# RWKV-6 attention and a gated MLP on one core: the first step's second chunk reads the first chunk by a seventh level

## The chip, the cores and the metric

The kernel runs on one core of a Trainium2 chip. Its time is the device time of one launch in microseconds (us); three runs of the kernel before gave 569.8 us as median, 569.65 at the lowest and 570.21 at the highest. The core has five engines with a queue of instructions each: TensorE (PE in the profile; its weight loads are PEld), VectorE (DVE), ScalarE (ACT), GpSimd (POOL), and SyncE (SP), which here issues DMA transfers. They wait for each other by semaphores only.

## The reference

Two blocks, one after the other. The attention has 4 sequences, 8 heads, 768 tokens and 48 channels a head, and carries a 48x48 state through the tokens:

```python
for t in range(S):
    cur = np.einsum('bhd,bhe->bhde', u[None] * kt, vt)
    y[:, :, t] = np.einsum('bhd,bhde->bhe', rt, state + cur)
    state = wt[:, :, :, None] * state + np.einsum('bhd,bhe->bhde', kt, vt)
```

Here rt, kt, vt and wt are token t of r, k, v and w, and the state starts at zero. The result, as 3072 rows of 384 numbers, goes through an MLP: `h = x @ w_in` (384 to 2048), `g = h * erf(softplus(h))`, and `g @ w_out` (2048 to 384). Everything is float32 here; a float32 matmul shows in the profile as two records.

## The kernel before

**Steps.** The work is cut into 12 steps. A step takes 128 tokens of two sequences, so 16 heads: r and k lie as `in[:, x, n]` (x = 0 for r, 1 for k), a tile of 128 partitions in which the even head e = 0 of pair n sits in partitions 0 to 47 and the odd head e = 1 in 64 to 111 (`rows(e)`), with the 128 tokens along the free dimension; n = 0 to 7, and j = 0, 1 is the sequence. The 128 tokens are two chunks of 64 (`HC`), called c or h = 0 and 1. In step 0 the tile is ordered by sequence first and read by `first_pair`.

**Levels.** Inside a chunk the decay between tokens s and t is built up by halves. At level l blocks of 2^l tokens are looked at: `level_products` (L712) multiplies k of every block's left half with r of its right half on PE into a PSUM bank (`pp`), `take_level` (L722, or L729 and L743 by ACT) moves the part that belongs to the level into the tile `own` (source token in the partitions, target token along the free dimension), and then `scale` (L357 and L364, DVE) multiplies r of the right halves by the total decay of the left halves and k of the left halves by that of the right halves, for the next level to use. POOL makes the totals (`plan_totals`, L397). Six levels finish a chunk of 64. PE's next level waits for the scaling of this one, and the scaling waits for this level's products, which read the same tile. `keep_busy` and `stay_warm` are matmuls whose results nobody reads.

**y and the state.** `from_own` (L756) multiplies `own` with v: a chunk's tokens over the same chunk, into the PSUM tile `y`. What chunk 1 takes from chunk 0 goes through the state: k is turned (transposes, L1023 in step 0, L1152 in the others), `state_part` (L829) multiplies the turned k with v, the result becomes `middle` (the state between the chunks), and `through_state` (L782) multiplies r of chunk 1 with `middle` into `y`. Then y is moved out: `y3` (L790), a matmul `hop` that puts the fourth part of y into free rows (L797, step 0), and copies into `xT` (L803). `xT` is what the MLP reads.

**The order in step 0 (`attend_first`, L950 to L1061).** After level 6, DVE scales k of both chunks (`scale_last(j, True)`, L374), PE turns k, then `from_own` of one half of y, ACT and DVE copy the turned k to `kT`, PE makes chunk 0's part of the state (`state_part(0, kT, ps, (0,))`), the other half of `from_own`, ACT and DVE copy it to `middle`, POOL fades it, PE runs `through_state`, ACT copies `y3`. Chunk 1's part of the state is made in step 1 by `pending`, between levels 2 and 3.

**Step 1 (`attend`, L1081).** Its PE order is written out: half of level 1, `hop`, the other half, then for each level a piece of the first step's MLP (L1242: two column blocks of x @ w_in, 12 records) after the level's products. The banks of PSUM for the products take turns (`products`, `turns["next"]`): level l + 1 uses the bank that level l - 1 used, and what `pending` writes at level l goes to the bank of level l + 1.

**The weights** come as 64-bit floats and are turned to 32 bits on the chip, in 16 pairs of rows: pair i is loaded into one of three buffers `words` ("l": two DMAs of 384 KB, SP; a small copy into the buffer, by ACT or POOL, sets when it may start), ACT makes the high part ("b", L289, for pairs 0 and 1 in PSUM tiles "m", of which there are two) and the low part ("r", L297), DVE shifts the high part ("h", L306) and POOL adds the two ("o", L319). Pair i of `w_in` must be ready for the i-th piece of L1242.

Everything around the change is issued in program order, engine by engine (a manual schedule); nothing is reordered.

## Time and profile before

| what | us |
|---|---|
| median of the three runs | 569.8 |
| the profiled execution's own time | 569.77 |
| its span | 568.0 |
| PE busy | 560.9 (99%) |
| DVE busy | 452.1 (80%) |
| ACT busy | 358.5 (63%) |
| POOL busy | 244.9 (43%) |
| DVE starts to scale behind level 6 of step 0 (L374) | 17.48 |
| `hop` starts (L797) | 23.08 |
| first MLP piece starts (L1242) | 25.26 |
| third MLP piece starts (L1242, in level 3 of step 1) | 33.62 |

The first three rows are times of a launch: the profiled execution took 569.77 us, 1.77 us more than the span in which its instructions lie. The busy rows are sums over that span. The last four rows are places in it, in us from its start, read from the chain of work that ended last: they follow the stretch that the change touches. PE is busy nearly everywhere; in the stretch from 17.9 to 22.6 us it was busy 3.92 of 4.70 us, from 25.3 to 48 us all the time.

### The profile page before, as it was taken

The numbers are of one execution on the slowest core, as the hardware profiler recorded it, in microseconds if no ns is written. First come the engines' busy times: TensorE is split into PE (matmuls) and PEld (weight loads), VectorE is DVE, ScalarE is ACT, GpSimd is POOL, SyncE is SP. The second block draws the span as 40 slices with busy tenths as digits, with TensorE's granted clock in tenths as the row PEclk, the third lists the DMA queues.
The fourth block names the chain that finished last, engine by engine and source line by source line (L and its number), as shares of the span: only waits on it lengthen the run. The fifth ranks groups of instructions, "written<-read, shape, count | busy, mean of one in ns | idle before, by whom it ended". The sixth has DMA issues, their size and how long they took to land.

```text
span 568.0 us, 16706 instructions
## 1 busy us (share of the span) xinstructions
PE 560.9 (99%) x7314; PEld 499.7 (88%) x7314; DVE 452.1 (80%) x511; ACT 358.5 (63%) x496; POOL 244.9 (43%) x262
## 2 busy tenths in 40 slices
PE   8999999999999999999999999999999999999997
PEld 6788886588988998998998998998899899989997
DVE  8895886999899898798798789689689487477720
ACT  3777787556458858747757766765676771589500
POOL 3785482533885883393484185176072000000000
PEclk9999999999999999999999999999999999999999
DMA  8793753350435325145145235235232201000000
GB/s 268 238 383 143 256 194 117 129 155 3 147 119 136 111 95 146 25 170 167 23 145 181 36 135 188 39 113 167 48 112 84 47 9 36 2 2 0 29 29 28
DMA packets 54081, 63.24 MB, mean 111 GB/s; under 512 B 35160, under 2 KB 40568, under 8 KB 52984
## 3 DMA queue, kind: packets, MB, share of 16 engines
q1 hardware_dynamic: 53480, 61.98, 34.5%
q8 instruction: 57, 0.93, 0.7%
q10 hardware_dynamic: 528, 0.20, 0.1%
q14 instruction: 16, 0.13, 0.1%
HBM read 52.39 MB, written 8.69 MB: 108 GB/s over the span
## 4 chain that ended last, share of the span: by engine, by line
PE 87%; DVE 7%; issue 3%; POOL 1%; ACT 1%; DVEq 0%; POOLq 0%; ACTq 0%
PE m L1364 33%; PE m L1242 31%; PE c L1467 6%; PE pp L712 5%; PE y L756 2%; PE m L1274 2%; PE y L782 2%; DVE in L364 2%; PE pp L829 2%; PE m L1067 1%; PE pp L1076 1%; POOL w_out_sb L1305 1%; DVE h L1207 1%; DVE own L722 1%; PE pp L1152 1%
## 5 line engine op out<-in xcount | busy, mean ns | idle before, releaser
L1242 PE MATMUL m<-xT,w_in_sb 128*128 128x256 f32 x960 | 214.6, 381 | 0.3 <-ACT h L1251 0.2
L1242 PEld LDWEIGHTS m<-xT,w_in_sb 128*128 128x128 f32 x960 | 180.1, 190 | 25.5 <-ACT h L1251 0.6
L364 DVE TENSOR_TENSOR in<-in,tot_sb 128x1024 f32<-128x1024 f32 (+1 forms) x55 | 77.5, 1409 | 6.6 <-PE pp L712 6.2
L1251 ACT COPY h<-m 128x512 f32<-128x512 f32 x80 | 46.2, 579 | 52.2 <-PE m L1242 52.0
L1364 PE MATMUL m<-mixed,h 128*128 128x192 f32 x320 | 56.7, 331 | 0.0
L1364 PE MATMUL m<-w_out_sb,h 128*128 128x192 f32 x320 | 56.1, 329 | 0.0
L1364 PEld LDWEIGHTS m<-mixed,h 128*128 128x128 f32 x320 | 51.8, 190 | 0.8
L1364 PEld LDWEIGHTS m<-w_out_sb,h 128*128 128x128 f32 x320 | 52.0, 190 | 0.5
L1364 PE MATMUL m<-w_out_sb,room 128*128 128x192 f32 x288 | 49.7, 326 | 0.0
L1364 PEld LDWEIGHTS m<-w_out_sb,room 128*128 128x128 f32 x288 | 47.3, 190 | 0.1
L1202 ACT ACT_TABLE_LOAD x28 | 35.9, 1283 | 8.7 <-DVE h L1207 6.7
L514 POOL TENSOR_TENSOR words<-words,own 128x384 f32<-128x384 f32 x21 | 29.8, 1418 | 26.3 <-DVE words L545 13.6
L712 PEld LDWEIGHTS pp<-in 48*48 48x48 f32 (+4 forms) x2368 | 30.2, 120 | 10.9 <-issue 6.0
L555 POOL TENSOR_TENSOR words<-words 128x384 f32<-128x384 f32 x28 | 38.7, 1410 | 0.0
L507 POOL TENSOR_TENSOR own<-rest 128x384 f32<-128x384 f32 x7 | 8.1, 1152 | 69.1 <-ACT o L1370 69.1
L1198 ACT ACT_TABLE_LOAD x28 | 35.9, 1283 | 1.8 <-issue 1.3
L712 PE MATMUL pp<-in 48*48 48x32 f32 (+4 forms) x2368 | 34.1, 206 | 0.2 <-DVE in L364 0.2
L459 POOL TENSOR_TENSOR tot_sb<-tot_sb 128x256 f32<-128x256 f32 (+4 forms) x50 | 30.9, 618 | 3.8
L580 DVE TENSOR_REDUCE sums<-rk 128x16 f32<-128x768 f32 (+2 forms) x31 | 31.3, 1022 | 0.0
L555 POOL TENSOR_TENSOR rk<-words 128x384 f32<-128x384 f32 x28 | 30.6, 1122 | 0.0
L1198 ACT ACTIVATE room<-h 128x1024 f32<-128x1024 f32 x28 | 29.6, 1057 | 0.3
L319 POOL TENSOR_TENSOR w_out_sb<-w_out_sb,rest 128x768 int32<-128x768 int32 x8 | 18.0, 2254 | 21.6 <-DVE w_out_sb L311 21.5
(222 smaller groups left out, 1007.0 us busy)
## 6 DMA issues: line engine op xcount, KB each, us to landing
in<-in_rkw SPq DMA_DIRECT2D x8, 1024.0 KB, 5.4
words<-in_moe_w_in SPq DMA_DIRECT2D x16, 384.0 KB, 6.0
words<-in_moe_w_out SPq DMA_DIRECT2D x16, 384.0 KB, 4.6
words<-in_rk_rows SPq DMA_DIRECT2D x8, 768.0 KB, 6.0
w<-in_rkw SPq DMA_DIRECT2D x11, 512.0 KB
v<-in_v SPq DMA_DIRECT2D x12, 384.0 KB, 5.6
out<-o SPq DMA_DIRECT2D x23, 192.0 KB, 4.0
in<-in_rkw SPq DMA_DIRECT2D x7, 512.0 KB, 5.7
```

The lines of the kernel that those rows point to most:

```text
L364: nc.vector.tensor_mul(halves, halves, view(tots[level - 1], 0, [[1, n], [2, nb], [0, half]]))
L459: nc.gpsimd.tensor_mul(new, pair[:, :, 0], pair[:, :, 1])
L514: engine.tensor_mul(to, to, of[:, :, None, :].to_broadcast([P, NEAR // 2 // half, half, D]))
L555: engine.tensor_mul(to[:, i], r[:, half:], k[:, part * rows + i, None].to_broadcast([P, half, D]),)
L580: nc.vector.tensor_reduce(out=to, in_=of, axis=mybir.AxisListType.X, op=ALU.add)
L712: nc.tensor.matmul(to, lhsT=rk(1, n)[rows(e), s0 : s0 + m], rhs=right, start=True, stop=True,)
L1198: nc.scalar.activation(sp_room, chunks[0], AF.Softplus)
L1202: nc.scalar.activation(at, sp_room, AF.Erf)
L1242: nc.tensor.matmul(ps[:, ff, :], lhsT=w_in_sb[:, g * FG + f + ff, kk * P : (kk + 1) * P], rhs=xT[:, kk, :], start=kk == 0, stop=kk == KT - 1,)
L1251: nc.scalar.copy(h[:, f : f + FT, :], ps[:])
L1364: nc.tensor.matmul(to, lhsT=a[:, f], rhs=b[:, f], start=start and f == 0, stop=f == FG - 1, skip_group_check=True,)
L1467: nc.tensor.matmul(to[:, f], lhsT=turns["weights"][b][:, i * FT + f], rhs=turns["tokens"][a], start=a + b in STARTS and not f, stop=True, ...
```

## The change

Step 0 no longer makes the state between its chunks. After level 6 it scales only what is needed next (k of chunk 0 for the first sequence, r of chunk 1 for all, k of chunk 0 for the second), and PE multiplies k of chunk 0 with r of chunk 1: a seventh level, 64x64 tokens for each of the 16 heads, into two "m" tiles (`far`), one for each e. `into_y` then takes the place of `from_own`, `state_part` and `through_state`: first y of chunk 0 over the 64 partitions of `own` that hold chunk 0; then DVE (e = 1) and ACT (e = 0) copy `far` over those 64 partitions, and y of chunk 1 is one matmul over all 128 partitions, chunk 0 and chunk 1 at once. k of chunk 1 is scaled behind that, and `move_last`, the second half of the old `through_state`, moves y out as before.

The transposes and both halves of the state go to step 1: at level 2 `pending` turns k and ACT copies it to `kT`; at level 3 it makes both halves of the state, DVE copies `middle`, POOL fades it, DVE adds the second half.

Weight pair 0 has its high part made in place in `w_in_sb`, in one instruction, so the "m" tiles are free for `far`. The loads of pairs 2 and 3 are set off by POOL instead of ACT: pair 2 behind level 6, pair 3 behind POOL's u products for step 1. `keep_busy` does three matmuls of 128 columns instead of one of 384, and `stay_warm` after level 1 does four of 128 instead of two of 256.

```diff
@@ -280,7 +274,9 @@
             if i not in held:
                 return
-            if i < 2:
+            if not i:
+                base = weights[i][0][:, part]
+            elif i < 2:
                 base = ps_m.tile([P, NP * C], FP32, name="m")[:, :DM]
             else:
                 base = y[:].rearrange("p e q j t -> p e (q j t)")[:, :, :DM]
...
@@ -365,15 +361,20 @@
             halves, halves, view(tots[level - 1], 0, [[1, n], [2, nb], [0, half]])
         )
-    def scale_last(batch, k):
-
-        half, nb = 1 << (LOG - 1), JP * C // NJ >> LOG
-        t, tots = turns["first"][:, batch], ready[0][1]
-        at, every, of = (NP * C, 1, 1) if k else (half + HC, NC, 2)
-        halves = view(t, at, [[2 * half * every, nb // every], [1, half]])
+    def scale_last(n, x, c):
+
+        half = 1 << (LOG - 1)
+        rk, tots = turns["first"], ready[0][1]
+        side = 1 - x
+        blocks = C // half
+        offset = (n.start // NP * 2 + x) * NP * C + n.start % NP * C + c * HC + side * half
+        many = n.stop - n.start > NP
+        dims = [[2 * NP * C, NJ], [C, NP]] if many else [[C, NP]]
+        halves = view(rk, offset, [*dims, [1, half]])
+        by = [[NP * blocks, NJ], [blocks, NP]] if many else [[blocks, NP]]
         nc.vector.tensor_mul(
             halves, halves,
-            view(tots[LOG - 1], 2 * batch * nb + of, [[2 * every, nb // every], [0, half]]),
+            view(tots[LOG - 1], n.start * blocks + NC * c + x, [*by, [0, half]]),
         )
     def plan_totals(s):
...
@@ -774,17 +775,21 @@
             if not (c or h):
                 continue
             t = slice(h * HC, (h + 1) * HC)
-            for j, q in ((0, 2), (1, 2), (1, 0), (0, 0)) if not s else np.ndindex(NJ, NP // 2):
-                q = q if not s else 2 * q
+            for j, q in np.ndindex(NJ, NP // 2):
+                q = 2 * q
                 for e in range(NE):
                     for p in (q + e, q + 1 - e):
                         n = j * NP + p
                         nc.tensor.matmul(
                             y[at(e, p), e, p // 2, j, t],
                             lhsT=state[rows(e), n, :],
-                            rhs=(in_t[:, 0, n] if s else first_pair(0, n))[rows(e), t],
+                            rhs=in_t[:, 0, n][rows(e), t],
                             start=False, stop=True, skip_group_check=True,
                         )
+
+        move_last(s, xT)
+
+    def move_last(s, xT):
         y3 = att.tile([P, UNIT], FP32, name="y3", bufs=1)
         nc.scalar.copy(y3[:].rearrange("p (j t) -> p j t", j=NJ), y[:, 1, 1])
...
@@ -961,7 +966,7 @@
         pp = products([P, NE, JP, HC])
         for half in halves:
             level_products(pp, by_pair(made), 1, half)
-        stay_warm(2)
+        stay_warm(4, 1)
         nc.scalar.copy(first[:], mask_sb[:, 0, :])
         for j in range(NJ):
             scale(0, 1, batch=j)
...
@@ -985,7 +990,7 @@
                 level_products(pp, first_pair, level, half)
                 scale(0, level, batch=j)
             turns["pp"] = products([P, NE, JP, HC])
-            keep_busy(turns["pp"], (DM,))
+            keep_busy(turns["pp"], (P,) * KT)
             (take_blocks if level == MASKED else take_level)(own, pp, level)
             wait_for(1 << level - 1)
             if level == 2:
...
@@ -993,8 +998,7 @@
             else:
                 totals(*behind[level])
             if level == 2:
-                stages["b"](0, 0)
-                stages["b"](0, 1)
+                stages["b"](0)
                 stages["r"](0)
                 nc.sync.dma_start(out=vt[:], in_=v[0])
             if level == 3:
...
@@ -1006,66 +1010,92 @@
                 nc.sync.dma_start(out=ws[1][:], in_=rkw[1][:, 2])
         totals = plan_totals(1)
         pp = turns.pop("pp")
-        for j, half in enumerate(halves):
+        all_n, (n0, n1) = slice(0, JP), (slice(j * NP, (j + 1) * NP) for j in range(NJ))
+        for half in halves:
             level_products(pp, first_pair, LOG, half)
-            scale_last(j, True)
-        got = pp[:].rearrange("p e n t -> p (e n) t")
-        half = HC // 2
-        for s0, copy in ((0, nc.scalar.copy), (HC, nc.vector.tensor_copy)):
-            copy(own[s0 : s0 + half, :, half:], got[s0 : s0 + half, :, :half])
+        scale_last(n0, 1, 0)
+        scale_last(all_n, 0, 1)
+        scale_last(n1, 1, 0)
+        far = [
+            ps_m.tile([P, NP * C], FP32, name="m")[:HC].rearrange("p (n t) -> p n t", n=JP)
+            for _ in range(NE)
+        ]
+        for n in range(JP):
+            for e in range(NE):
+                nc.tensor.matmul(
+                    far[e][:, n, :], lhsT=first_pair(1, n)[rows(e), :HC],
+                    rhs=first_pair(0, n)[rows(e), HC:], start=True, stop=True,
+                )
+        take_level(own, pp, LOG)
+        stages["l"](2, ready[0][1][LOG - 1][:, 0:1])
         wait_for(0, 1)
         next(second)
-
-        kT = att.tile([P, NH, D], FP32, name="kT", bufs=1)
-        turned = products([P, JP, P])
-        turns["next"] = 1 - turns["next"]
-        for n in range(JP):
-            nc.tensor.transpose(turned[:, n, :], first_pair(1, n), ident[:])
-        from_own(0, own, 1)
-        for e, copy in ((1, nc.scalar.copy), (0, nc.vector.tensor_copy)):
-            copy(kT[:, e * JP : (e + 1) * JP], turned[:, :, e * EP : e * EP + D])
-        for j in range(NJ):
-            scale_last(j, False)
-        fence()
-        stages["l"](2, seen[:, 0:1], True)
-        ps = [[products([P, NE, JP, HC], 1 - e)[:, e] for e in range(NE)]]
-        state_part(0, kT, ps, (0,))
-        from_own(0, own, 0)
-        nc.scalar.copy(middle[rows(1)], ps[0][1][rows(1), :, :D])
-        nc.vector.tensor_copy(middle[rows(0)], ps[0][0][rows(0), :, :D])
-        stages["l"](3, middle[:, 0, 0:1], True)
+        scale_last(all_n, 1, 1)
+
+        def into_y(h, e):
+
+            t = slice(h * HC, (h + 1) * HC)
+            of = slice(0, t.stop) if h else t
+            for j, q in np.ndindex(NJ, NP // 2):
+                for p in (2 * q, 2 * q + 1):
+                    n = j * NP + p
+                    nc.tensor.matmul(
+                        y[at(e, p), e, q, j, t],
+                        lhsT=vt[of, n * NE + e, :], rhs=own[of, e * JP + n, :],
+                        start=not (h or j or q), stop=True, skip_group_check=True,
+                    )
+
+        for e, copy in ((1, nc.vector.tensor_copy), (0, nc.scalar.copy)):
+            into_y(0, e)
+            copy(own[:HC, e * JP : (e + 1) * JP], far[e])
+        into_y(1, 1)
+        into_y(1, 0)
+        stages["l"](3, ready[1][0][:, 1, 0, 0:1])
         load_v(1)
         stages["h"](0)
-        stages["h"](0)
-        nc.gpsimd.tensor_mul(faded[1][:], middle[:], ends[:, :, 1:2].to_broadcast([P, JP, D]))
-        stages["o"](0)
-        through_state(0, xT)
         stages["b"](1, 0)
+        move_last(0, xT)
         stages["b"](1, 1)
         stages["r"](1)
+        stages["o"](0)
         stages["h"](1)
         stages["h"](1)
         totals(1)
         stages["o"](1)
         totals(2)
         turns["totals"] = lambda: totals(*range(3, LOG + 1))
-
-        def pending():
-            part = products([P, NE, JP, HC], turns["next"])[:, 0]
-            state_part(0, kT, ps + [[part] * NE], (1,))
-            nc.vector.tensor_add(S_next[both], faded[1][both], part[both, :, :D])
-            load_third()
-            stages["l"](5)
-            load_w(2)
+        kT = att.tile([P, NH, D], FP32, name="kT", bufs=1)
+
+        def pending(level):
+            if level == 2:
+                turned = products([P, JP, P], turns["next"])
+                for n in range(JP):
+                    nc.tensor.transpose(turned[:, n, :], first_pair(1, n), ident[:])
+                nc.scalar.copy(
+                    kT[:].rearrange("p (e n) d -> p e n d", e=NE),
+                    turned.rearrange("p n (e d) -> p e n d", e=NE)[..., :D],
+                )
+                loaded[2] = [ins.tile([P, 2, JP, C], FP32, name="in"), None]
+                stages["l"](5)
+                load_w(2)
+                return
+            both_halves = products([P, NC, JP, HC], turns["next"])
+            state_part(0, kT, [[both_halves[:, h]] * NE for h in range(NC)])
+            nc.vector.tensor_copy(middle[both], both_halves[both, 0, :, :D])
+            nc.gpsimd.tensor_mul(
+                faded[1][:], middle[:], ends[:, :, 1:2].to_broadcast([P, JP, D])
+            )
+            nc.vector.tensor_add(S_next[both], faded[1][both], both_halves[both, 1, :, :D])
+            loaded[2][1] = ins.tile([P, NH, D], FP32, name="v")
         turns["pending"] = pending
-    def stay_warm(times):
+    def stay_warm(times, wide=NC):
         for _ in range(times):
-            ps = ps_m.tile([P, NC, P], FP32, name="m")
+            ps = ps_m.tile([P, wide, P], FP32, name="m")
             nc.tensor.matmul(
-                ps[:], lhsT=ident[:], rhs=ident[:, None, :].to_broadcast([P, NC, P]),
+                ps[:], lhsT=ident[:], rhs=ident[:, None, :].to_broadcast([P, wide, P]),
                 start=True, stop=True,
             )
...
@@ -1105,8 +1135,8 @@
             if s == 1 and 2 < level:
                 stages["h"](level + 1)
             scale(s, level)
-            if s == 1 and level == 2:
-                turns.pop("pending")()
+            if s == 1 and level in (2, 3):
+                turns["pending"](level)
             if s == 1 and level == 2:
                 stages["h"](3)
             if s == 1 and level > 1:
```

## The prediction

> **What bounds the kernel now.** I read the page's busy shares first, then a table by stretches of time, then the chain that ended last around the change, then the timelines of DVE and POOL there.
>
> ```profile
> PE 560.9 (99%) x7314; PEld 499.7 (88%) x7314; DVE 452.1 (80%) x511; ACT 358.5 (63%) x496; POOL 244.9 (43%) x262
> ```
>
> PE is the bound: 7.1 us of 568.0 are left. So a change can gain only where PE idles, or by PE work that it takes away.
>
> ```profile
> 17.90:22.60 4.70, 3.92 (x150) 3.45 (x153) 3.64 (x10) 1.91 (x6) 2.69 (x6) 1.00 0.51 130
> 22.60:25.30 2.70, 2.69 (x71) 2.04 (x62) 1.93 (x4) 2.65 (x7) 2.70 (x3) 1.00 0.80 251
> 25.30:36.40 11.10, 11.10 (x200) 9.20 (x200) 9.67 (x10) 7.59 (x13) 9.51 (x11) 1.00 0.99 360
> 36.40:48.00 11.60, 11.60 (x263) 9.63 (x263) 9.94 (x9) 8.85 (x16) 10.22 (x11) 1.00 0.99 389
> ```
>
> The columns are the stretch, its length, then busy time of PE, PEld, DVE, ACT, POOL, the granted clock (1.00) and the DMA share. In the stretch that the change rewrites PE idles 0.78 us; where the state is to go it never idles, and DVE hardly does.
>
> The chain that ended last:
>
> ```profile
> 17.48 0.44 DVE in L374
> 17.92 0.14 issue
> 18.05 1.08 PE pp L1023 x8
> 19.16 0.49 ACT kT L1026
> 19.67 0.57 DVE kT L1026
> 20.28 0.88 PE pp L829 x30
> 21.25 0.54 DVE middle L1035
> 21.93 0.67 PE y L782 x32
> 22.60 0.47 PE pp L712 x32
> 23.08 1.56 PE y L797 x6
> ...
> 29.09 0.73 PE pp L829 x32
> ...
> 47.90 1.02 PE pp L1152 x8
> ...
> 51.52 0.86 PE pp L829 x64
> ```
>
> From level 6 to hop the work passes from engine to engine: turn, copy, state, copy, y. Behind hop the chain is PE alone. The rows at 47.90 and 51.52 are step 1's own transposes and state, and price the moved ones.
>
> ```profile
> 29.22 2.61 DVE L364 TENSOR_TENSOR in<-in,tot_sb 128x1024 f32<-128x1024 f32 x1 [0.98 <-PE pp L712]
> 31.75 0.54 DVE L1056 TENSOR_TENSOR s<-faded,pp 112x384 f32<-112x384 f32 x1
> 33.31 1.84 POOL L319 TENSOR_TENSOR w_in_sb<-w_in_sb,rest 128x768 int32<-128x768 int32 x1
> 35.13 1.19 DVE L364 TENSOR_TENSOR in<-in,tot_sb 128x1024 f32<-128x1024 f32 x1
> ```
>
> These set the waits in the new place: level 3's scaling, after which the new copy to middle stands, ended at 36.32, and the next PE level began at 36.41.
>
> **The change, part by part.** The sum goes against the profiled execution: span 568.0, its own time 569.77, 1.77 around it; the median of the runs shown is 569.80.
>
> *The path to hop.* Rates from the trace: the half state at 20.28 uses two quarters of the array and takes 27.5 ns a record at 48 columns (0.88/32), 37 at 64 by ratio; y by the state (L782), in four quarters, 21 ns at 64 columns (0.67/32). The full state in four quarters takes 13.4 ns at 48 columns (0.86/64), so two quarters cost twice four; single records start in pairs 45 ns apart at 48 columns, hence 56 to 60 at 64: 28 a record, the value I take.
> DVE: k of chunk 0, first sequence, 17.48, 0.31 (L374's 128-element form, 0.62 for two); r of chunk 1 waits for the second half of level 6 and ends at 18.35 (0.42, the 256-element form); k of the second sequence 18.66. PE starts far at 18.5 (0.14 hand-over, the row at 17.92): 32 records x 28 = 0.90, 19.40. The copy of level 6 into own, now two on ACT at 0.58 each from 17.93, is done by then. into_y of chunk 0, e = 1: 16 records, 0.45, 19.85; its last record drains in 0.2 and DVE copies from 20.05 to 20.70 (L1015's copy of 512 columns, 0.69, and 0.55 for 384). e = 0 runs meanwhile on PE to 20.30 and on ACT 20.50 to 21.08. into_y of chunk 1: 20.85, twice 0.45, 21.75; half of level 1, 0.47; hop at 22.3 with a switch of the array's form. Before: 23.08. **-0.8.** y3 (0.37 on ACT) runs beside the last into_y, after pair 1's first high part (0.54): its words were sent for at 13.62, and SP's transfers up to it were moved by 20 us. The deferred k of chunk 1 (0.42 on DVE, 18.66) and POOL's u products (1.84, from 18.8) are done by 21.0, ahead of level 1.
>
> No trace row has a matmul over all 128 rows with 48 columns out. Its bounds are 28 ns a record (two column halves side by side, as the half state has in 64 rows) and 54 (a quarter of the 215 ns between starts of L1242's 256-column records: one after the other), so 0.45 or 0.86 each; I take the first, the row nearest in shape. The Trainium skill, "TensorEngine Tiling (Array Packing)", Tiling Modes, lists 128 rows by 64 columns as two independent tiles, and under Key Properties says that changing the mode drains the array: by the first 0.45 stands, by the second each switch costs. The switch shows here too: last transpose at 18.85, next y record at 19.05 against 0.11 between transposes, so 0.1; two of them, one under the wait for DVE's copy.
>
> *PE work put into step 1.* Transposes 1.02 and full state 0.86, less the half state that stood there, 0.73: **+1.15**, all on the path, since nothing idles there.
>
> *Waits in step 1.* Add the two: hop to the third piece took 10.54 (23.08 to 33.62), so level 3's products come at 32.1 and end at 33.1. The state needs the bank of level 2: DVE's level 2 scaling starts 28.45 (0.8 earlier), 2.53 to the next; its add of 0.5 is gone; shift 0.86, level 2's take ends 33.15. Wait 0.1. Then DVE: shift, level 3's scaling ending 35.05, middle 0.56 (L1176's form) to 35.6, POOL fades 0.83 to 36.45, add 0.54 to 37.05. Level 4's products go to the bank which that add reads: PE arrives at 36.9 and waits until 37.1. **+0.3** together, bounded by 0 (DVE 0.4 earlier) and 1.9 (the fade behind one POOL add of 1.84). Behind the add, DVE has the take of level 3, a shift and level 4's scaling, 0.7 + 0.9 + 1.2, ending at 39.9; PE wants it at 40.9. DVE's stall while POOL fades (0.9) is covered by that 1.0; without it level 5 would wait.
> Of DVE's 2.61 at 29.22 against 1.19 at 35.13 the difference is POOL, busy through the first and idle in the second. The Trainium skill, "SBUF — State Buffer", Who interferes with whom, says that a DVE instruction with two SBUF inputs and a GpSimd one that reads SBUF exclude each other: the trace agrees. Were POOL's adds shifted clear of that scaling, the 0.3 would be 0 and the sum 570.1.
>
> *At nothing.* The kT copy (0.80, L1154's form) falls into ACT's idle 2.2 between 31 and 33 and has PE's 2.79 of MLP to finish under; without it level 3 waits 0.8. Pair 0's high part in one instruction (0.89 for 1.07) and one shift (0.96 or less for 1.00) lie before the first piece, 0.6 clear on POOL's add. keep_busy and stay_warm keep their columns: 6 records of 128 at 108 ns (the spacing of weight loads at 7.65) are 0.65 for 2 of 384 at 0.32; if each took a full weight load (0.19) it would be +0.3, but level 6's second half waits for DVE until 17.4 anyway. SP sends pair 2 near 18.2 instead of 21.09, behind w of step 1 (17.36), pair 3 near 21, v behind it: all earlier, and no PE wait in this stretch was for weights. The load queue is full from 25 to 45, but pairs 2 to 7 were added 2.3 us or more before their pieces. The third step's tiles are claimed later, still ahead of their transfers at 31.68.
>
> **Sum:** -0.8 + 1.15 + 0.3 = +0.65; 569.77 + 0.65 = 570.4 us.
>
> **Rivals.**
> *Full-row matmuls one after the other* (slower side). 0.86 for 0.45, twice: +0.8, 571.2. It decides from 44 ns a record on (0.5 over 32 records, which takes the sum past +0.2%). For it: no such row before. Against: the half state pairs its column halves in shared rows.
> *The two copies of far do not run side by side.* DVE's copy of own waited for ACT's (18.54, L1015) and again at L1026, both from one PSUM tile; here there are two tiles, as in L1034 and L1035, which overlapped. If they queue: +0.7, 571.1.
> *The fade stands behind POOL's add of pair 3.* That add began at 33.31 and would now begin near 32.5; from 34.3 on it delays the fade beyond +0.5. Then up to +1.5: about 571.3.
> *No waits, quicker head.* DVE's copy at 0.56, far at the four-quarter rate of 16 ns (0.5 for 0.9): hop -1.3, waits 0: 569.6, no change.
> *Moved work is free* (faster side). If transposes and state fell into waits of PE, hop alone would count: -0.8 to -1.3, 568.7. Against: the stretch table shows none.
>
> **How the numbers follow.** A difference of 0.2% is 1.14 us, about what a measurement of this kernel can tell from no change. Forecast 0.53 (its own range 569.9 to 570.9); full rows 0.13; copies 0.07; POOL 0.07; quicker head 0.14; free 0.06, of which 0.05 goes past 0.2%. Slower by over 0.2%: the three together, 0.27; faster 0.05; within 0.68. The range takes in the quicker head below, 569.3, and above the rivals' 571.1 to 571.3 with 0.3 for the waits' upper bound, 571.6; what is left out is the free case, 0.06, and the ends of the others, 0.1.
>
> **What would show it.** hop near 22.3; far in pairs 56 ns apart and into_y of chunk 1 at 28 ns a record, not 54; the third MLP piece near 34.1, not 33.62; two L829 rows gone from step 0 and one of 64 records before that piece; a PE wait on DVE's add of the state ahead of level 4; from 45 us on every PE row late by one amount, 0.4 to 0.9. If hop comes before 21.5, or the third piece before 33.5, I have missed idle time of PE; if lateness changes behind step 1, a wait that I do not see.

## The result, and the profile after

The changed kernel takes 576.34 us (median of 6 runs, 571.94 to 578.91), the kernel before 569.78 in the runs beside it (569.64 to 570.21): a ratio of 1.011, with a 95% interval of 1.0072 to 1.0147. It is slower by some 6.6 us, ten times the 0.65 of the forecast's sum, and outside the range of 569.3 to 571.6. The profiled execution took 575.78 us with a span of 574.0, so 6.0 more than the 568.0 before. Of the runs of the next section, two of the kernel before (822.88 and 960.33 us) and one of e6 (579.98) were in a slow state and are left out of the ratios.

The first lines to compare are the page's busy shares, the granted clock in 40 slices, and the DMA queue that the page calls "instruction", of the changed kernel, with the clock of the kernel before as the last line:

```profile
PE 564.8 (98%) x7334; PEld 506.0 (88%) x7334; DVE 449.5 (78%) x508; ACT 359.1 (63%) x494; POOL 243.5 (42%) x264
PEclk9699999999999999999999999999999999999999
q8 instruction: 57, 0.93, 0.7%
PEclk9999999999999999999999999999999999999999
```

PE is busy 3.9 us longer, and its idle time grew from 7.1 to 9.2 us. Only 20 records were added, so most of that growth is records that became longer. The second digit of the clock, which stood for full speed before, is a 6. The third line is the same before and after; its use comes below.

The table by stretches of 5 us of the changed kernel, with the columns of the prediction's table (stretch, length, PE, PEld, DVE, ACT, POOL, clock, DMA share, and GB/s last):

```profile
15.00:20.00 5.00, 3.29 (x141) 2.84 (x140) 3.41 (x8) 3.37 (x10) 1.83 (x7) 0.83 0.76 263
20.00:25.00 5.00, 4.98 (x93) 4.79 (x93) 1.78 (x4) 1.42 (x3) 3.28 (x6) 0.50 0.88 254
25.00:30.00 5.00, 5.00 (x81) 3.95 (x78) 2.13 (x4) 2.56 (x6) 4.49 (x4) 0.65 0.38 150
30.00:35.00 5.00, 5.00 (x88) 4.32 (x87) 3.30 (x4) 4.45 (x7) 3.15 (x3) 1.00 0.71 244
40.00:45.00 5.00, 3.77 (x77) 3.05 (x76) 2.85 (x4) 2.27 (x3) 2.73 (x3) 1.00 1.02 404
```

The clock is 0.50 throughout 20 to 25 us and back at 1.00 by 30. PE idles 1.7 us in the first stretch and 1.2 in the last, and the last belongs to level 4 of step 1, where the prediction found PE never idle. The chain that ended last says what the idle time waited for:

```profile
15.12 0.79 PE pp L713 x55
15.90 1.18 issue
17.08 0.29 PE pp L713 x9
...
18.24 0.99 PE pp L713 x64
19.23 0.02 issue
19.25 0.44 DVE in L375
19.69 0.04 issue
19.73 1.65 PE m L1025 x26
...
21.70 1.76 PE y L1042 x29
...
23.48 1.95 PE y L1042 x32
25.43 1.06 PE pp L713 x32
26.50 2.52 PE y L802 x6
...
38.83 2.79 PE m L1272 x12
41.61 0.53 PE pp L713 x28
42.15 1.23 issue
43.38 0.70 PE pp L713 x33
44.08 2.79 PE m L1272 x12
46.87 0.85 PE pp L713 x64
```

For nothing that the profile shows: both pauses are "issue". Each stands inside a run of equal matmuls (level 5 of step 0, 55 records before and 9 after; level 4 of step 1), where no semaphore is waited for. The kernel before runs both levels in one piece:

```profile
14.96 1.02 PE L712 MATMUL pp<-in 48*48 48x32 f32 x64
36.38 1.03 PE L712 MATMUL pp<-in 48*56 48x32 f32 x64
```

Between the pauses the records are long: hop (L802) takes 2.52 us against 1.56, one half of into_y 1.76 to 1.95.

The places below are starts in PE's timeline. "Late" is against the kernel before; the last columns are two experiments of the next section that keep the new order without the first pause.

| place | before | after | late | e1 | e6 |
|---|---|---|---|---|---|
| level 6 of step 0 | 16.89 | 18.17 | 1.28 | 17.49 | 16.82 |
| hop | 23.08 | 26.43 | 3.35 | 23.25 | 22.49 |
| third MLP piece | 33.55 | 38.76 | 5.21 | 34.56 | 33.79 |
| level 4 of step 1 | 36.38 | 41.55 | 5.17 | 37.76 | 36.95 |
| level 5 of step 1 | 40.12 | 46.80 | 6.68 | | |
| last record of PE | 564.59 | 570.60 | 6.01 | | |

From the table the 6.68 us split into: 1.28 by the first pause; 3.52 by the half clock (level 6 to hop 8.26 against 5.76 in e1, hop to the third piece 12.33 against 11.31); 0.78 by the new order (e1, from level 6 to level 4, 20.27 against 19.49 before); less 0.41, because PE is so late that it no longer waits ahead of level 4 (2.79 from the third piece against 3.20 in e1); and 1.51 by the second pause (the last step of the lateness, 6.68 - 5.17). About 0.7 is won back between 58 and 142 us. (e1 starts 0.6 late at level 6 because its level 1 began at 7.09, against 6.51: the first full clock in its trace begins at 7.80, against 5.75, and its warm-up matmuls still follow each other at 0.43 us where those of the kernel before do at 0.22.)

**What a pause is.** Of queue 8 the page counts 57 packets and 0.93 MB, 16 KB each. PE has 7,314 weight loads and as many matmuls in the kernel before: 0.93 MB by 14,628 is 64 bytes for each, so a packet holds 256 instructions, and 57 packets hold 14,592, nearly all of them. I read queue 8 as PE's own instructions. Counted in the trace, the two pauses of the changed kernel fall ahead of PE's weight loads number 350 and 859: 509 apart, four times 127, and 127 pairs of load and matmul are a packet, less a few instructions that are no matmul. In the changed kernel a packet starts at 14.79 and PE resumes at 17.08; another at 40.75, resumed at 43.38. The DMA view of 14.7 to 15.9 us shows the packet among the others:

```profile
q1 hardware_dynamic: 90, 0.26, 82.6%
q8 instruction: 1, 0.02, 5.1%
```

The other queue fills the engines to 82.6% meanwhile. In the 19 pauses of this kind of 0.6 us or more, here and in the runs below, PE resumes 2.21 to 2.63 us after the start of such a packet. Before the change PE reached its 350th weight load 2.38 us after its packet started, and did not stop; the load lay 6 records into level 6, behind a keep_busy. The new fillers hold 16 more records up to there (eight instead of four in stay_warm, six instead of two in each of three keep_busys), so that the 350th falls 56 records into level 5, which runs at about 16 ns a record, and is reached at 15.68, 0.9 after the packet's start.

The Trainium skill, "Runtime: NRT & Kernel Launch", Instruction fetch mechanics, says that an engine's sequencer refills its instructions in 16 KiB blocks of 256 over a DMA queue of its own, which agrees with the 57 packets. It also says that the refill is hidden by the pace at which instructions are dispatched: here it is not, where records follow at 16 ns.

### The profile page after: what moved, and what is told of

The parts are those of the page before. It is cut to its first block, busy times and chain, and to the rows that moved or that the text cites. A ratio compares the mean times of both kernels' runs of the same rounds, so it can differ in the third digit from the quotient of the medians.

```text
span 574.0 us, 16742 instructions
## 1 busy us (share of the span) xinstructions
PE 564.8 (98%) x7334; PEld 506.0 (88%) x7334; DVE 449.5 (78%) x508; ACT 359.1 (63%) x494; POOL 243.5 (42%) x264
## 4 chain that ended last, share of the span: by engine, by line
PE 93%; DVE 4%; ACT 1%; issue 1%; DMA 1%; DVEq 0%; ACTq 0%
PE m L1272 35%; PE m L1394 33%; PE pp L713 6%; PE c L1497 6%; PE m L1304 4%; PE y L757 2%; PE y L783 2%; PE pp L834 2%; DVE in L360 1%; DMA in<-in_rkw 1%; PE pp L1182 1%; PE y L1042 1%; PE pp L1106 1%; DVE h L1237 1%; PE c L1394 0%
## 5 line engine op out<-in xcount | busy, mean ns | idle before, releaser
L360 DVE TENSOR_TENSOR in<-in,tot_sb 128x1024 f32<-128x1024 f32 (+1 forms) x55 | 74.5, 1355 | 10.9 <-PE pp L713 9.0
```

Of the source, the lines that this page charges most:

```text
L360: nc.vector.tensor_mul(halves, halves, view(tots[level - 1], 0, [[1, n], [2, nb], [0, half]]))
```

## The experiments

The theory after the result: the fillers' added records make the first pause, and the pause makes the clock drop; the new order itself costs what was forecast. The rivals: the new order makes the pauses (through the weights' loads that it moves); or the fillers cost by what they compute. Each run's time is read beside its mean granted clock, because a stretch of half clock is 3.41 us long and takes 0.003 off that mean: "at full clock" means 0.999 or more. The kernel before, beside the experiments, had a median of 570.1 at full clock on each chip, and 17 of 92 runs were below full clock.

**The new order with the old fillers, and one of the two fillers.**

```diff
-        stay_warm(4, 1)
+        stay_warm(2)                        # e1 only
-            keep_busy(turns["pp"], (P,) * KT)
+            keep_busy(turns["pp"], (DM,))   # both
```

> The changed kernel with the old fillers: keep_busy again one matmul of 384 columns, stay_warm again two of 256. Seen in the changed kernel: PE pauses 1.4 us at 15.7 us, in the middle of level 5's products, with nothing to wait for, while a 16 KB packet of the instruction queue has just landed; the clock is 0.5 from 18.3 to 28.5 us. Theory A (supply of instructions): the smaller fillers lengthen PE's instruction stream by 16 matmul records up to level 5, so that the 350th weight load, where the pause is, falls inside a run of dense products; with the old fillers it falls at the start of level 6 as in the kernel before, there is no pause at 15.7, the clock stays at 1.0, and the time is about 570.4 us, as predicted. Theory B (the new order itself lets the clock drop, by its idle PE ahead of the seventh level): the clock still drops near 18 us and the time stays near 576.

> The changed kernel with the old keep_busy alone; stay_warm stays at four matmuls of 128 columns (4 records more than before). Theory A: the 350th weight load lies 2 records into level 6, behind a filler: no pause, clock 1.0, the time of the run with both old fillers within 0.3 us. A third possibility (the fine filler itself, not its count of instructions, lets the clock drop): also no drop here, so it is not told apart by this run but by the one with narrow matmuls ahead. Theory B: near 576 us.

Measured: e1 572.48 (571.55 to 577.71, 10 runs), ratio 1.0049 [1.0022, 1.0076]; e3 573.48 (570.73 to 578.39), 1.0058 [1.0030, 1.0087]. At full clock 571.91 (6 of 10) and 571.56 (4 of 10), where the changed kernel reached full clock in 2 of 16 runs, at 571.94 and 572.25. PE's timeline of e1:

```profile
23.25 1.56 PE L802 MATMUL y<-y,mixed 128*128 128x256 f32 x6
...
29.20 1.09 PE L1073 MATMUL pp<-ident,in 128*128 128x128 f32 x8
...
33.71 0.91 PE L834 MATMUL pp<-v,kT 64*48 64x48 f32 x64
34.56 2.86 PE L1272 MATMUL m<-xT,w_in_sb 128*128 128x256 f32 x12
37.76 0.82 PE L713 MATMUL pp<-in 48*56 48x32 f32 x48 [0.34 <-DVE s L1088]
40.18 0.41 PE L713 MATMUL pp<-in 48*56 48x32 f32 x16 [1.60 <-issue]
```

The first pause and the half clock in the head are gone, in both runs; the second pause is not, and it is again at the 859th weight load, although that is now the 49th record of level 4 instead of the 29th. e3's second pause costs it the clock, from 40.44 to 43.85:

```profile
39.20 0.50 PE L713 MATMUL pp<-in 48*56 48x32 f32 x20 [1.45 <-issue]
```

So the first pause is made by the fillers, keep_busy above all, and the second needs only the new order. Neither version came down to the 570.4 expected, because of that second pause. The two runs of the changed kernel at full clock are hardly later than e1's 571.91: as far as two runs tell, the fillers' price is paid almost wholly through the clock.

**The fillers alone, in the kernel before.**

```diff
-        stay_warm(2)
+        stay_warm(4, 1)
-            keep_busy(turns["pp"], (DM,))
+            keep_busy(turns["pp"], (P,) * KT)
```

> The kernel before with only the new fillers: keep_busy three matmuls of 128 columns, stay_warm four of 128; nothing of the seventh level. Theory A: the pause of 1.2 to 1.4 us comes in level 5's products and the clock drops in most runs: 572 to 577 us, spread over several us. Theory B: 569.8 us as before, clock 1.0.

Measured: 571.70 (570.06 to 576.74, 10 runs), ratio 1.0042 [1.0011, 1.0074]; 570.63 at full clock (5 of 10). PE's timeline:

```profile
16.46 0.82 PE L712 MATMUL pp<-in 48*48 48x32 f32 x55
19.04 0.30 PE L712 MATMUL pp<-in 48*48 48x32 f32 x9 [1.75 <-issue]
```

The same pause at the same place, 55 records and 9, without the new order and with its weight loads unmoved. The trace also has pauses of 0.85 at weight load 222 and 0.48 at 732. The granted clock is at half from 20.75 to 24.16. The median is 1.5 us above the kernel before, just under the 572 to 577 expected. This leaves the rival of the moved loads out for the first pause.

**The stream shifted without either.** Eight matmuls of 8 columns at the very start of the kernel before move every place by 16 records:

```diff
+        more = ps_m.tile([P, P], FP32, name="m")
+        for _ in range(8):
+            nc.tensor.matmul(more[:, :8], lhsT=ident[:], rhs=ident[:, :8], start=True, stop=True)
```

> The kernel before with eight matmuls of 8 columns (16 records) put at the very start, where PE warms up; fillers and everything else as before. It shifts the stream of instructions by as much as the small fillers do up to level 5. Theory A: the pause comes in level 5's products, the clock drops in most runs, 572 to 577 us. If the small fillers matter by themselves: no pause, 569.8 to 570.2 us. Theory B: 569.8 to 570.2 us.

Measured: 574.35 (570.94 to 577.65, 10 runs), ratio 1.0054 [1.0023, 1.0085]; 571.10 at full clock (4 of 10), and 6 of 10 with stretches of half clock. The profiled run shows a pause of 0.64 at the 222nd weight load, one packet earlier than I had expected, and none at the 350th. It does not settle much: the eight matmuls themselves took 1.85 us (6.54 to 8.32) and put level 6 at 18.68, 1.8 late, so the stream met other packets at other times. It shows that a pause can be moved to another edge, not that the shift alone makes the loss. That the count of the fillers' instructions matters, and not their form, is therefore argued from the places of the pauses and not shown by a run of its own.

**Shifting the stream back, and taking PE's waits away.** Four versions of e1 were to remove the second pause or the order's waits. e5 repeats the products of two pairs in level 1, 16 records that write the same values again; e6 puts the state ahead of level 3's scaling and DVE's add behind it; e7 makes the transposes in step 0, between the halves of into_y, where PE waits for DVE; e8 is all three.

```diff
 # e5, in level 1 of step 1
+                level_products(pp, rk, level, range(NP, NP + 2))
 # e6
+            if s == 1 and level == 3:
+                turns["pending"](3)
             scale(s, level)
...
-                turns["pending"](level)
+                turns["pending"](2 * level - 2)   # level 4: DVE's add alone
 # e7, behind into_y(0, e) of both e
+        turned = products([P, JP, P], 1 - turns["next"])
+        for n in range(JP):
+            nc.tensor.transpose(turned[:, n, :], first_pair(1, n), ident[:])
         into_y(1, 1)
```

> The changed kernel with both old fillers, and in step 1's level 1 the products of two pairs done twice (16 records more, about 0.25 us, result the same). With the old fillers alone the profile has a pause of 1.6 us at the 859th weight load, 49 into level 4 of step 1. Theory A (PE runs out of instructions at fixed places of its stream, every 127 weight loads, when a run of dense products lies ahead of one): the 859th now lies 33 into level 4 with the slow MLP piece just ahead of it, so the pause goes, or shrinks below 0.5 us; undisturbed runs at 570.4 to 571.0 us instead of 571.6 to 572.8, and fewer runs with a clock below 0.999 than 4 in 10. If the pause belongs to the work itself (level 4 waiting on something that the profile does not show): it stays at 1.6 us in the middle of level 4, 571.8 to 573 us.

> The changed kernel with both old fillers; in level 3 of step 1 the state's products, the copy to middle and POOL's fade go ahead of DVE's scaling, only the add behind it, so that DVE does not stand still while POOL fades and the bank of level 4 is free about 1 us earlier. Theory A with the supply of instructions held up behind PE's wait for that bank (with the old fillers the packet of instructions began at 37.73, level 4 at 37.76, when the add was done): the packet begins about 1 us earlier, the pause at the 859th weight load shrinks from 1.6 to 0.4 to 0.8 us, PE's wait of 0.3 for the add goes: undisturbed runs near 570.7 us. If the packet's time does not hang on that wait: the pause stays at 1.6, 571.5 us.

> The changed kernel with both old fillers; the transposes of k stay in step 0, between the two halves of into_y, where PE waited 0.8 us for the copies of far; ACT copies kT behind the hop. Takes 1.0 us of PE work out of step 1 and adds 0.1 to 0.3 ahead of hop: 0.7 to 0.9 us below the run with the old fillers alone, if the moved PE work is on the path as the sum has it; level with it, if the moved work was free. The pause at the 859th weight load stays: undisturbed runs 570.8 to 571.2.

> All three together: products of two pairs done twice, the add behind the scaling, the transposes in the gap. By the sum: hop -0.3 against the kernel before, state +0.13, the doubled products +0.25, no pause: 569.6 to 570.1 us undisturbed, level with the kernel before; clock at 1.0 in nearly all runs. If the new head lets the clock drop by itself: several runs of ten below 0.999.

| run | median, us (lowest, highest; runs) | ratio | at full clock | pauses in the profiled run, at weight load |
|---|---|---|---|---|
| e5 | 572.24 (570.54, 577.58; 10) | 1.0038 [1.0006, 1.0071] | 571.55 (6) | 0.5 at 350, 1.3 at 477, 1.4 at 859 |
| e6 | 575.02 (571.37, 579.98; 4) | 1.0102 [1.0042, 1.0162] | 571.37 (1) | 0.85 at 859 |
| e7 | 572.64 (571.52, 579.43; 10) | 1.0045 [1.0008, 1.0082] | 571.81 (7) | 0.8 at 350, 1.8 at 477, 1.7 at 859 |
| e8 | 572.93 (570.73, 577.50; 10) | 1.0049 [1.0020, 1.0078] | 571.40 (6) | 0.7 at 859; 1.6 at 1379 |

At full clock they stand 0.1 to 0.5 under e1. None lost the pause at 859, and the times expected of them were missed: at full clock each is 0.5 us or more above. But the place of that pause follows the count and not the work: it comes ahead of record 25 of level 4 in e11 below, 29 in the changed kernel, 33 in e5, 45 in e3 and 49 in e1. In all the profiled runs PE's pauses of this kind (0.3 us or more, in the first 75 us) lie at loads 222, 350, 477, 732 and 859, to one record, each time behind the first, second, third, fifth and sixth packet of queue 8. The 1379th, in e8, is no such edge: there the trace has PE wait for a semaphore, from 61.63 to 63.69, until a DMA has landed, although the timeline calls it "issue" too; the other pauses have no such record. The clock fell at 63.80, right behind it.

```profile
63.75 4.51 PE L1282 MATMUL m<-xT,w_in_sb 128*128 128x256 f32 x12 [1.57 <-issue]
```

e7 is level with e1: the transposes in PE's gap won nothing that shows, and its profiled run stops at two packets' edges for longer than the 0.93 that they take, so it does not decide whether the moved work was free. e6 is the clearest view of the order itself, since its level 6 starts within 0.1 us of the kernel before (16.82 and 16.89). PE's timeline of e6:

```profile
16.82 0.91 PE L713 MATMUL pp<-in 48*32 48x32 f32 x64
...
20.81 1.12 PE L1042 MATMUL y<-own,v 128*48 128x64 f32 x32 [0.49 <-DVE own L1050]
...
22.49 1.56 PE L802 MATMUL y<-y,mixed 128*128 128x256 f32 x6
...
33.79 2.86 PE L1278 MATMUL m<-xT,w_in_sb 128*128 128x256 f32 x12
36.95 0.82 PE L713 MATMUL pp<-in 48*56 48x32 f32 x48 [0.30 <-DVE s L1083]
38.62 0.41 PE L713 MATMUL pp<-in 48*56 48x32 f32 x16 [0.85 <-issue]
```

The add behind the scaling did not take PE's wait ahead of level 4 away (0.30), but the pause behind it fell from 1.60 to 0.85: its packet started at 36.10, 0.85 ahead of level 4, where e1's started at 37.73, 0.03 ahead.

**The pause without the change's order.** Does idle time of PE alone drop the clock? In the kernel before ACT multiplies the zeros that keep_busy reads by 1.0 some more times, at level 5 of step 0: PE is held by a semaphore, and its stream is as before. e9 holds it by two such instructions, e12 by five.

```diff
+            if level == MASKED:
+                for _ in range(2):   # e12: 5
+                    nc.scalar.mul(out=states[1][0][:], in_=states[1][0][:], mul=1.0)
```

> The kernel before, its PE stream unchanged; at level 5 ACT multiplies the zeros that keep_busy reads by one, twice, so that PE waits about 1.4 us near 16 us for an engine instead of for its instructions. If a pause of PE there is what lets the clock drop: a run of ten or several have a clock of 0.991 to 0.997 and 573 to 577 us, the others are at 571.0 to 571.6 us (the pause alone). If the clock drop needs more than the pause (the new order, the small fillers): clock 1.0 as often as in the kernel before, all near 571.3 us.

> As the kernel before with PE held near 16 us, but by five multiplications on ACT instead of two, which with two held PE for 0.77 us, cost 0.6 us and left 6 of 10 runs at a clock of 1.0 (the others at 0.996 or 0.997). Each multiplication is 0.45 us, so PE waits about 2.1 us, longer than the pauses of 1.2 to 1.8 us for instructions. If an idle PE of that length is what lets the clock drop, whatever it waits for: most of ten runs have a clock below 0.999, and they are 1.7 us later for every 0.003; the others at 571.6 to 572.2 us. If the clock drop belongs to the supply of instructions or to the new order alone: clock 1.0 in about four of five runs, as in the kernel before, and all of those near 571.9 us.

Measured: e9 570.76 (570.27 to 572.80, 10 runs), ratio 0.9985 [0.9957, 1.0013], with 570.39 at full clock (6 of 10); e12 573.98 (573.06 to 574.82), 1.0029 [1.0001, 1.0058], and none of its 10 runs at full clock (0.993 to 0.997). Both ratios are against runs of the kernel before of which many had stretches of half clock themselves (6 of 25 and 5 of 13); the medians at full clock tell more. PE's timeline of e9:

```profile
16.86 0.91 PE L1079 MATMUL pp<-s,ident 128*128 128x384 f32 x2 [0.77 <-ACT s L990]
```

and of e12, followed by its table by stretches:

```profile
18.62 1.65 PE L1079 MATMUL pp<-s,ident 128*128 128x384 f32 x2 [2.09 <-ACT s L990]
```

```profile
15.00:20.00 5.00, 2.91 (x68) 1.40 (x66) 2.84 (x5) 4.78 (x12) 2.06 (x6) 0.79 0.78 194
20.00:25.00 5.00, 4.61 (x119) 3.76 (x120) 2.45 (x7) 1.05 (x2) 1.96 (x4) 0.53 0.19 74
```

Held 0.77 us, PE lost 0.25 us at full clock and kept the clock in 6 of 10 runs; held 2.09 us it lost the clock every time. So idle time of PE is enough to drop the clock, without the fillers, the new order or a missing instruction. e9 says little by itself, since the kernel before lost the clock in 6 of 25 runs beside it. The changed kernel's pauses of some 1.2 us lie between the two lengths; that one of them is enough rests on e2, at half clock in 5 of 10 runs with the pause, where the kernel before was in 2 of 31.

**Again, and once more, meant to be without a pause.** e10 is the changed kernel itself, e11 is e6 with three pairs' products repeated in level 2 of step 1 (24 records), placed so that the 859th weight load should fall among the slow MLP records.

```diff
+                if s == 1 and level == 2:
+                    level_products(pp, rk, level, range(3))
```

> The changed kernel itself, beside the others on one chip. Theory A: pauses at the 350th and the 859th weight load again, 1.2 to 1.6 us each; runs with a clock of 1.0 at 571.9 to 573 us (0.5 for the new order, 2.4 for the pauses), the others 1.7 us later for every 0.003 of the clock, 574 to 579 us; more than half of the runs with a clock below 0.999.

> The changed kernel with both old fillers, the add behind the scaling, and in level 2 of step 1 the products of three pairs done twice (24 records, 0.35 us): the 859th weight load now lies 25 into level 4, with the whole of the third MLP piece between it and the state's products, where the fetch should be sent for. Theory A: no pause in level 4; undisturbed runs at 570.3 to 570.9 us (569.8, 0.5 for the new order, 0.35 for the doubled products), so 0.7 us below the run with the add behind the scaling alone, doubled products and all; a clock below 0.999 about as often as in the kernel before. If the pauses come from the loads of data that run at the same time: a pause of about 1 us is still there in level 4.

Measured: e10 575.52 (572.25 to 579.85, 10 runs), ratio 1.0079 [1.0043, 1.0116], one run of ten at full clock, and pauses of 1.18 at the 350th, 1.03 at the 477th and 0.89 at the 859th weight load in its profiled run, with half clock from 24.06 to 27.47 behind the second; e11 571.76 (570.86 to 577.62), 1.0025 [0.9992, 1.0058], seven at full clock, 571.20 there. e11's profiled run still pauses, 0.4 at the 350th, 1.3 at the 477th and 0.6 at the 859th: the aim was missed, though its median is the lowest of the versions with the new order. By the ratio it can't be told apart from the kernel before, at full clock it is 1.05 later (571.20 against 570.15); no version beat that one. Its half clock began at 21.68, ahead of the pause at the 477th (21.72) and behind the small one at the 350th and PE's two waits of 0.5, for the scaling and for the copies of far. So the rival may have a part: the new order's own waits seem to cost the clock at times, though e1 kept it behind the same two waits.

## Why the prediction was wrong

**The step that failed** stands under "At nothing": "keep_busy and stay_warm keep their columns". I priced these edits by columns and by the cost of a weight load, and found cover for both. The cost came in by the number of instructions: 16 more records shift PE's stream against the edges of its 256-instruction packets, one edge falls into dense products, and PE runs dry there. e2 shows it in the kernel before, e1 and e3 show it by its absence. The second assumption that went with it was the granted clock of 1.00: with the first pause it fell to 0.50 for 10.24 us, 3.52 us of time. The fillers are not the whole of it: e1, without them, is still 1.8 us above the kernel before at full clock (571.91 against 570.14) and above the range, and most of that is the second pause. What failed is wider than the two fillers: the sum had PE's instructions always at hand. By the table the first pause, the half clock and the second pause are 6.3 of the 6.7 us; the clues were in the page before (queue 8's 57 packets), and I read them as nothing.

**The sum for the order came out, in part by luck.** From level 6 to level 4 the new order costs +0.64 (e6: 20.13 against 19.49) to +0.78 (e1), where the prediction had -0.8 + 1.15 + 0.3 = +0.65. Its terms were each off, and the errors cancel: the head won 0.3 to 0.4 less, the moved work cost 0.4 less, the wait 0.1 to 0.2 more. And the second pause stands right behind level 4, outside this stretch.

- The path to hop: -0.43 (e1) to -0.52 (e6) instead of -0.8. far took 0.93 from its first record's start to its last's (e1: 18.98 to 19.91), for 0.90, and into_y of chunk 1 starts 4.0 after level 6 in both runs, as forecast (20.85 against 16.89). What was short stands behind it: into_y over 128 rows takes 1.05 until level 1 starts (e6: 20.81 to 21.86) for 0.9, and the half of level 1 takes 0.63 until hop starts, for 0.55 with the switch in it.
- Work put into step 1: hop to the third piece takes 11.3 in both runs against 10.47, so +0.84 instead of 1.15 and 0.1, and no wait for level 2's bank shows. The transposes took 0.93 (29.20 to 30.13 in e1) instead of 1.02, the full state 0.85; the half state that they replace had taken 0.83 from start to start (28.92 to 29.75), not the 0.73 of the chain, whose row begins only at 29.09.
- The wait ahead of level 4: it came where it was said, on DVE's add (L1088), and the third piece to level 4 takes 3.16 to 3.20 against 2.83: +0.33 to +0.37, for 0.2.

**The rivals.** Full-row matmuls one after the other: false; in e1 the records over 128 rows start in pairs, eight of them in 0.223 us at their densest, so 28 ns a record (31 over all 32), as the row nearest in shape said. The Trainium skill's two independent tiles of 128 rows by 64 columns ("TensorEngine Tiling (Array Packing)", Tiling Modes) agree with that. The two copies of far ran side by side (e1: DVE 20.68 to 21.36, ACT 21.13 to 21.71). The fade began right behind the copy to middle, so POOL's add of pair 3 did not hold it. The quicker head did not come. Moved work was not free.

**What would show it.** The state's two rows are gone from step 0 and one of 64 records stands ahead of the third piece (e1, L834). The prediction said that from 45 us on every PE row would be late by one amount, and that a lateness which changes behind step 1 would mean a wait that I do not see. Lateness is 6.68 at level 5 and 6.01 at the end; the waits I did not see stood ahead of that.

**What stays open.** Why the packet of the 859th weight load starts so late in the changed kernels: PE is then 27 to 49 weight loads from the edge, before it was 56. Its start falls within 0.15 us of the end of DVE's add of the state in three kernels (e1 37.73 and 37.70, e3 36.96 and 36.83, e7 42.37 and 42.22) but up to 1.2 us ahead of it in the others (after 40.75 and 41.43, e11 40.65 and 41.85), so the add isn't its cause by itself. Whether the load queue, full at those moments before and after, delays the packet was not tried. That the packet carries the very instructions at which PE stops is inferred from the counts and the order of the packets.

## What to carry to other kernels

Count PE's instructions as well as its work when an edit touches small matmuls: at some 16 ns a record a stream eats a packet of 127 loads and matmuls in about 2 us, and PE went on 2.2 to 2.6 us after a packet's start. An "issue" pause inside a run of equal matmuls is to be looked for at equal distances of 256 instructions, once a semaphore is ruled out; an edit far ahead of it can move it there or away. Judge the price of about a microsecond of idle PE by the granted clock behind it, and over several runs, since it falls or not with the moment.

## What the hardware did that was not expected

The granted clock fell to half behind pauses of 1.0 to 2.1 us, in e11 behind two of 0.5, and for whole multiples of 3.41 us: 18.30 to 28.54 in the changed kernel (three), 20.75 to 24.16 in e2 (one). Whether it falls varies from run to run of one kernel: 14 of 16 runs of the changed kernel, 5 of 10 of e2, 10 of 10 of e12, 4 of 10 of e9 with 0.77 us of waiting. The Trainium skill, "TensorE: Matmul & The Clock Gate", Part 1, gives a free-running window of 3413 ns: the lengths agree. It has the clock fall after at least one idle window: the idle time here was three to six tenths of one. In each profiled run the clock's changes lie on one grid of 3.41 us, whose place differs from run to run. Away from the kernel's start and end, PE was idle for 1.02 to 2.08 us in the ten stretches of that grid ahead of a fall, but also for 1.01 to 1.60 in six that had none behind them; so the amount in a stretch alone does not decide, and what else does stays open.

The refill of PE's instructions took 2.21 to 2.63 us from the packet's start to PE's next record in 19 pauses; in the changed kernel the load queue was busy beside it. The kernel before stood at this edge already: 2.38 us at the 350th weight load. That would explain its own runs below full clock, but none of these was profiled.
